# Clustered attention and its feed-forward layer on one core: rows of probabilities normalised before the float16 split instead of after the product with the values

## The chip, the cores and the metric

The kernel runs on one core of a Trainium2 chip. Its measure is the device time of one launch in microseconds (us); three runs of the kernel before gave 845.54, 847.42 and 848.62 us, a median of 847.42 us. Beside the timed runs there is one execution that was taken with the hardware profiler.

The core has five engines that run side by side, each through a queue of its own in a fixed order: TensorE (PE, matrix products; PEld is its loading of weights), VectorE (DVE), ScalarE (ACT), GpSimd (POOL) and SyncE (SP, which only issues DMAs here). An instruction that needs another engine's result waits on a semaphore, and all that is queued behind it on its engine waits with it.

## The reference

Four batches with 8 heads, 768 tokens and 64 features per head go through an attention in which a query sees only the keys of its own cluster, and then through a feed-forward layer of width 2048.

```python
q_assign = np.argmax(einsum(q / (norm(q) + 1e-6), c / (norm(c) + 1e-6)))   # 16 clusters per head; k_assign alike
scores = scale * q @ k.T                                                    # scale = 64 ** -0.5
scores = np.where(q_assign == k_assign, scores, -1e9)
attn = np.exp(scores - scores.max(-1))
attn = attn / (attn.sum(-1) + 1e-9)
x = attn @ v                                                                # heads side by side: 3072 x 512
h = x @ w_in                                                                # 512 x 2048
g = np.where(h >= 1, h, np.where(h <= -1, 0, (h + 1) ** 2 / 4))
out = g @ w_out                                                             # 2048 x 512
```

## The kernel before

**Tiling.** Queries go in 12 units u: batch b (4) times chunk c (3 chunks of 256 queries). A unit has 4 pairs of heads (hp), and a pair has 4 score steps n (2 heads times 2 tiles of 128 queries). A score step is four products of 128x384 on TensorE into the PSUM tile `pair0`: two of queries by keys, two that add a large penalty where the clusters differ (`at_scores`). VectorE takes the 128x768 scores out of PSUM with the row's bound in the same pass (`sS<-pair`, followed by a short read of its accumulator, `sbi`).

**Softmax.** In `at_soft`, ScalarE computes the exponential of those 768 columns in place and its row sum (`rs`), and then casts the result to float16 (`hl[:, 0]`); GpSimd subtracts this from the float32 values and so gets the lower half (`hl[:, 1]`). A DMA transposes both halves into `pT`. The very first unit keeps float32 and transposes on TensorE (`whole`). The three buffers of `sS` are used in turn, and so are three of `hl` and three of `pT`.

**Sum rows.** The row sums are applied after the product with the values. When the four sums of a pair of heads are there, `at_sums` takes 1/(sum + 1e-9) on ScalarE and VectorE and splits it in two float16 columns on GpSimd (`rr`). In `at_av`, eight small products of 128 columns on TensorE (`banka<-idu,rr`) spread these columns over the partitions into half of the PSUM bank `bank_a`, and 36 products of 256 columns (`banka<-pT,kv`) form attention times values in the other half. ScalarE copies the spread sums out (`rb<-banka`), VectorE multiplies the two (`rb<-banka,rb`), ScalarE casts the result to float16 (`X[u][:, 0]`), and GpSimd subtracts for the lower half (`X[u][:, 1]`). X is what the feed-forward products read; its buffers are named x, wk and word.

**Phi.** Queries and keys are scaled by powers of two before their float16 split. In `q_pairs`, four short VectorE instructions find a bound and a factor phi that brings the queries of a pair of heads in line with it; GpSimd multiplies the natural queries by phi (`qn<-qn,phi`) and ScalarE the transposed ones (`q<-q,phi`), each once per pair of heads and unit, 48 times in all.

**Feed-forward.** A unit has 8 groups f: 24 products of 256 columns into one of three PSUM banks (`bankh`, `banki`, `bankj`), two VectorE passes of 512 columns, a square, a cast and a subtraction on ScalarE and GpSimd, and 12 products of 512 columns into `pair1`. The groups of one unit run between the attention of later units.

**Norm of the centroids.** At the start `centroids` takes the norm with ScalarE's square root, and a tiny exponential behind it brings the table of the exponential back for all that follows.

**What sets the order.** The code records every instruction with a step; `Recorder.issue` turns this into one order by a planner: a backward pass gives each instruction a priority, a table of numbers (`NUDGES`) changes these, and `forward` then plays the engines with prices for each instruction and writes the order out. So the order of the instructions on all engines is fixed when the kernel is built, and a change of the code or of the table moves instructions everywhere.

Of the kernel before, what the change touches and what calls it, by code (L numbers as in the profile page):

```python
# [9 lines left out]
F16 = mybir.dt.float16  # L10
# [14 lines left out]
UNIT = 2.0**-10  # L25
EXP_MASK2 = 0x7F000000
# [20 lines left out]
BASE = 20  # L47
NUDGES = (
# [56 lines left out]
)  # L105
TILED = 248

def mix(a):  # L110

    a &= 0xFFFFFFFF
    a ^= a >> 16
    a = a * 0x7FEB352D & 0xFFFFFFFF
    a ^= a >> 15
    a = a * 0x846CA68B & 0xFFFFFFFF
    return a ^ a >> 16
# [1348 lines left out]
```

## Time and profile before

| | |
|---|---|
| median of three runs | 847.42 us (845.54 to 848.62) |
| span of the profiled execution | 844.9 us |
| PE busy | 807.8 us, 96% |
| PEld busy | 563.2 us, 67% |
| ACT busy | 667.1 us, 79% |
| DVE busy | 628.9 us, 74% |
| POOL busy | 528.7 us, 63% |
| granted clock of TensorE, mean | 0.994 |

The profiled execution has no timed value of its own in the answers: its span from the first to the last instruction is 844.9 us, 2.5 us under the median of the timed runs and inside a microsecond of the fastest. Work outside the span and the scatter of the runs lie in that difference.

How to read the rows below: a group names what an instruction writes and what it reads by the program's tile names (out<-in), with the number of partitions and elements. "busy" is the union of its time, "mean ns" the mean duration of one. Two instructions of one engine can overlap by some tens of ns, so durations add up to more than the busy time of the engine. Nearly all instructions stand under one line, since one helper issues them; the tile names tell them apart.

### The profile page before, as it was taken

Reading aid. Unit: us, or ns where it says so; the run is one execution under the profiler, and the core shown is the slowest. Engines: PE = TensorE matmul, PEld = TensorE weight load, DVE = VectorE, ACT = ScalarE, POOL = GpSimd, SP = SyncE. Lnnn points to the kernel's source line nnn. Section 1 sums busy time; section 2 is a strip of 40 time slices with the busy share of each in tenths; the row PEclk is TensorE's granted clock in tenths of the full one; section 3 lists DMA queues with packets and bytes.
Section 4 is the critical chain, followed back from the end, with each engine's and each line's share of the span. In section 5 each row is a group of like instructions: output and inputs, shape, how many; then the busy total and the mean of one; then the engine's idle time right before and its main releaser. Section 6 shows DMA issues by size and latency. Waiting matters only on the chain.

```text
span 844.9 us, 18910 instructions
## 1 busy us (share of the span) xinstructions
PE 807.8 (96%) x7100; PEld 563.2 (67%) x7100; DVE 628.9 (74%) x1390; ACT 667.1 (79%) x1175; POOL 528.7 (63%) x510
## 2 busy tenths in 40 slices
PE   2677999999999999999999999999999999999998
PEld 2455677667676767666666767666676676667776
DVE  5999998788888758669888758678888767454331
ACT  7889999999988778788778778788778778776332
POOL 1012589888878668666667667666757668666312
PEclk9999999999999999999999999999999999999999
DMA  9977898979999799889999979999988767666100
GB/s 313 295 187 179 241 225 192 182 156 198 207 170 183 149 160 175 173 181 207 203 159 179 157 149 175 188 189 193 212 161 145 154 135 141 129 128 103 24 26 26
DMA packets 404907, 142.50 MB, mean 169 GB/s; under 512 B 372816, under 2 KB 396624, under 8 KB 404816
## 3 DMA queue, kind: packets, MB, share of 16 engines
q1 hardware_dynamic: 404816, 141.30, 82.0%
q8 instruction: 55, 0.90, 0.4%
q14 instruction: 36, 0.29, 0.1%
HBM read 40.40 MB, written 6.29 MB: 55 GB/s over the span
## 4 chain that ended last, share of the span: by engine, by line
PE 85%; DVE 6%; issue 2%; DMA 1%; ACT 1%; POOL 1%; SPq 0%; DVEq 0%; POOLq 0%; ACTq 0%
PE pair L405 42%; PE banka L405 12%; PE bankj L405 11%; PE banki L405 11%; PE bankh L405 9%; DVE sS L405 1%; DMA kv<-n 1%; DVE w L405 1%; DVE bankj L405 1%; DMA pT<-hl 1%; POOL hl L405 0%; DVE wk L405 0%; DVE x L405 0%; DVE mx L405 0%; DVE bankh L405 0%
## 5 line engine op out<-in xcount | busy, mean ns | idle before, releaser
L405 POOL TENSOR_TENSOR hl<-sS,hl 128x768 f16<-128x768 f32 x176 | 299.0, 1702 | 118.3 <-ACT hl L405 99.0
L405 PE MATMUL pair<-w,g 128*128 128x512 f16 (+2 forms) x1120 | 275.9, 387 | 0.0
L405 DVE CUSTOM_DVE_ANT_0 sS<-pair,zero,er 128x768 f32<-128x768 f32 x192 | 194.4, 1013 | 71.5 <-PE pair L405 57.7
L405 PEld LDWEIGHTS <-w 128*128 128x128 f16 x2112 | 205.6, 98 | 41.2 <-issue 2.0
L405 ACT ACTIVATE sS<-sS,sbi 128x768 f32<-128x768 f32 x192 | 179.1, 933 | 67.5 <-DVE sbi L405 64.9
L405 PEld LDWEIGHTS <-g 128*128 128x128 f16 x1104 | 105.5, 98 | 101.8 <-issue 1.4
L405 PE MATMUL pair<-kv,q 128*128 128x384 f16 x768 | 159.7, 332 | 5.6 <-ACT pT L405 3.3
L405 ACT CAST hl<-sS 128x768 f16<-128x768 f32 x176 | 144.7, 826 | 7.8 <-DMA pT<-hl 5.6
L405 POOL TENSOR_TENSOR g<-r,g 128x512 f16<-128x512 f32 x80 | 95.8, 1198 | 54.7 <-ACT g L405 54.5
L405 PEld LDWEIGHTS <-q 128*128 128x128 f16 x992 | 78.7, 98 | 62.8 <-issue 20.4
L405 PE MATMUL banka<-pT,kv 128*64 128x256 f16 (+1 forms) x1680 | 104.8, 279 | 0.0
L405 PEld LDWEIGHTS <-kv 128*64 128x64 f16 (+1 forms) x1824 | 92.6, 108 | 6.5 <-DMA kv<-n 2.6
L405 ACT ACTIVATE r<-r,f_ra,f_rs 128x512 f32<-128x512 f32 x80 | 64.8, 810 | 25.4 <-DVE r L405 24.8
L405 PE MATMUL bankj<-x,w 128*128 128x256 f16 (+1 forms) x424 | 58.3, 289 | 0.9 <-DVE r L405 0.9
L405 ACT CAST g<-r 128x512 f16<-128x512 f32 x80 | 48.9, 611 | 8.1 <-DVE r L405 7.1
L405 POOL TENSOR_TENSOR qn<-qn,phi 128x256 f16<-128x256 f16 x48 | 31.7, 676 | 36.3 <-DVE phi L405 27.2
L405 PE MATMUL bankh<-x,w 128*128 128x256 f16 (+1 forms) x376 | 46.7, 277 | 0.0
L405 PE MATMUL banki<-x,w 128*128 128x256 f16 (+1 forms) x288 | 40.0, 290 | 0.0
L405 ACT ACTIVATE q<-q,phi 128x512 f16<-128x512 f16 x48 | 33.6, 717 | 5.0 <-DVE phi L405 4.9
L405 PE MATMUL banki<-wk,w 128*128 128x256 f16 x312 | 37.2, 273 | 0.0
L405 ACT ACTIVATION_READ_ACCUMULATOR sS<-sS,sbi 128x1 f32 x192 | 36.1, 188 | 0.0
L405 POOL CAST rr<-rs 128x4 f16<-128x4 f32 x48 | 13.2, 276 | 36.1 <-DVE bankh L405 13.7
(269 smaller groups left out, 1114.8 us busy)
## 6 DMA issues: line engine op xcount, KB each, us to landing
w<-in_moe_w_out_dram SPq DMA_DIRECT2D x14, 512.0 KB, 5.8
q<-in_q_dram SPq DMA_DIRECT2D x12, 512.0 KB, 4.8
kv<-in_k_dram SPq DMA_DIRECT2D x16, 384.0 KB, 4.3
kv<-in_v_dram SPq DMA_DIRECT2D x16, 384.0 KB, 4.6
out_dram<-o SPq DMA_DIRECT2D x11, 512.0 KB, 3.6
w<-in_moe_w_in_dram SPq DMA_DIRECT2D x10, 512.0 KB, 7.3
word<-in_moe_w_in_dram SPq DMA_DIRECT2D x6, 512.0 KB, 6.0
o<-in_v_dram SPq DMA_DIRECT2D x8, 384.0 KB, 4.0
```

The costliest lines, as they stand in the source:

```text
L405: fn(*args, **kw)
```

## The change

Four things are done, and the planner's table is another one.

- **Batches 1 to 3, softmax** (`at_soft`): behind the exponential, ScalarE scales the one row sum of this step (128x1), VectorE takes its reciprocal (128x1) and multiplies the 768 float32 probabilities by it in place (`NORM = "dddd"` gives all four steps of a pair to VectorE); only then come the float16 cast on ScalarE and the subtraction on GpSimd. The factor 2^15 (`WIDE`) is taken out again behind the product.
- **Batches 1 to 3, values** (`at_av`): no sums per pair (`at_sums`), no eight spreading products. ScalarE writes `X[u][:, 0]` straight from PSUM, and VectorE writes `X[u][:, 1]` as the product less that. `PAIRS = 1` leaves one pair of heads per call, as before. Batch 0 stays as it was.
- **Chunks 1 and 2 of every batch** (`q_scale`, `q_pairs`): no phi. The bound goes into the scale of the queries by two short VectorE instructions in `q_scale`, and one VectorE copy (128x16x64 float16) takes the place of the phi products. Chunk 0 of each batch keeps phi, so 16 of the 48 products on each of GpSimd and ScalarE stay.
- **Centroids**: the norm comes from three Newton steps on VectorE (128x1 each), and the exponential's table is loaded at once, so one table load is left.
- **Buffers**: `wk` and `word`, which serve the weights early on, become one tile `late`; from batch 1 on, two more buffers for `pT` lie in it, five in all. The ring of X has four buffers where it had seven.
- **Order**: `NUDGES` and its hash go, `SHIFTS` adds one number per recorded call to the priorities, and the backward pass is repeated 31 times instead of 20.

```diff
-BASE = 20
-NUDGES = (
...
+WIDE = 2.0**15
+NORM = "dddd"
+PAIRS = 1
+BASE = 31
+SHIFTS = (
+    -300, 6196, 4613, 9761, -1686, 3724, 8146, 5319, 7315, -16432, -1123, 6379, -15621, -10423, -3454, 2074, -3225,
...
-        for seed in NUDGES:
-            self.nudge(seed, prio)
+        names = sorted({x.ev for x in self.nodes})
+        shift = dict(zip(names, SHIFTS, strict=True))
+        for x in self.nodes:
+            prio[x] += shift[x.ev]
...
-    wk = tiles("wk", 2, 4096)
-    word = tiles("word", 1, 8192)[0]
-    rings["w32"], rings["x"] = Ring(wk[:1] + rings["o"].bufs), Ring(tiles("x", 3, 4096) + wk + [word[:, :1024], word[:, 1024:]])
+    late = tiles("late", 1, 16384)[0]
+    wk, word = [late[:, :1024], late[:, 1024:2048]], late[:, 2048:]
+    rings["w32"], rings["x"] = Ring(wk[:1] + rings["o"].bufs), Ring(tiles("x", 3, 4096) + [late[:, 3072:]])
...
-    rec.scalar.activation(out=tab, in_=ones[:, :1], func=AF.Sqrt)
+    rec.scalar.activation(out=tab, in_=ones[:, :1], func=AF.Exp, scale=0.0)
...
-        nrm = const.tile([P, 1], F32, name="c_nrm")
-        rec.scalar.activation(out=nrm, in_=ss, func=AF.Sqrt)
-        rec.scalar.activation(out=tab, in_=nrm, func=AF.Exp, scale=0.0)
-        rn = const.tile([P, 1], F32, name="c_rn")
-        rec.vector.tensor_scalar(out=rn, in0=nrm, scalar1=1e-6, scalar2=None, op0=ALU.add)
+        (rn, y), m = (const.tile([P, 1], F32, name=f"c_{x}") for x in ("rn", "y")), tab
+        rec.vector.tensor_scalar(
+            out=y.bitcast(U32), in0=ss.bitcast(U32), scalar1=-0.5, scalar2=float(0x5F3759DF), op0=ALU.mult, op1=ALU.add
+        )
+        for _ in range(3):
+            rec.vector.scalar_tensor_tensor(out=m, in0=y, scalar=ss, in1=y, op0=ALU.mult, op1=ALU.mult)
+            rec.vector.tensor_scalar(out=m, in0=m, scalar1=-0.5, scalar2=1.5, op0=ALU.mult, op1=ALU.add)
+            rec.vector.tensor_tensor(out=y, in0=y, in1=m, op=ALU.mult)
+        rec.vector.tensor_scalar(out=rn, in0=ss, scalar1=y, scalar2=1e-6, op0=ALU.mult, op1=ALU.add)
...
+        if u % NCH:
+            f = BX[u // NCH]
+            es = e["es"] = new("es", [NP], F32, 2)
+            rec.vector.scalar_tensor_tensor(
+                out=iv, in0=f["sk"], scalar=ES_MIN / QK, in1=iv, op0=ALU.mult, op1=ALU.max
+            )
+            rec.vector.scalar_tensor_tensor(
+                out=es, in0=f["ik"], scalar=-QK, in1=iv, op0=ALU.mult, op1=ALU.mult
+            )
...
-        raw, es, ri = (ps[:, i * NP : i * NP + m] for i in range(3))
+        if c:
+            es = e["es"][:, pairs]
+            rec.vector.tensor_copy(nat[:, x, 0], nat[:, x, 1])
+        else:
+            raw, es = (ps[:, i * NP : i * NP + m] for i in range(2))
...
-            e["pT", j] = new("pT", [2 * T, CT, P], F16, 3)
+            new("pT", [2 * T, CT, P], F16, 3)
+            if b:
+                if "late" not in rings:
+                    rings["late"] = Ring(rings["pT"].bufs + [late[:, :1536], late[:, 1536:3072]])
+                rings["late"].i += 1
+                e["pT", j] = view(rings["late"].last(), [2 * T, CT, P], F16)
+            else:
+                e["pT", j] = view(rings["pT"].last(), [2 * T, CT, P], F16)
...
+        if b:
+            r = e["rs"][:, n : n + 1]
+            rec.scalar.activation(out=r, in_=r, func=AF.Copy, scale=1 / WIDE, bias=1e-9 / WIDE)
+            rec.vector.reciprocal(r, r)
+            who = NORM[n]
+            if who == "d":
+                rec.vector.tensor_scalar(out=sf, in0=sf, scalar1=r, scalar2=None, op0=ALU.mult)
+            elif who == "a":
+                rec.scalar.activation(out=sf, in_=sf, func=AF.Copy, scale=r)
+            else:
+                rec.gpsimd.tensor_tensor(out=sf, in0=sf, in1=r.to_broadcast([P, S]), op=ALU.mult)
-        at_sums(e, n)
+        if not b:
+            at_sums(e, n)
...
-    def at_av(b, hp, c):
-        pv, rb = bank_a[:, :CQ], bank_a[:, CQ:]
+    def at_av(b, hps, c):
+        u, n = b * NCH + c, len(hps)
+        es, kvs = [A.pop((b, hp, c)) for hp in hps], [KV[b, hp] for hp in hps]
+        pv = bank_a[:, : n * CQ].rearrange("p (n q) -> p n q", q=CQ)
+        rb = bank_a[:, CQ:].rearrange("p (n q) -> p n q", q=CQ)
+            for x, e in enumerate(() if b else es):
+            for x, (e, kv) in enumerate(zip(es, kvs)):
-        rs = new("rb", [CQ], F32)
...
+        to = slice(hps[0], hps[-1] + 1)
+        if hps[0] == 0:
+            X[u] = new("x", [NP, CQ], F32) if u == 0 else new("x", [2, NP, CQ], F16)
+        if b:
+            rec.scalar.activation(out=X[u][:, 0, to], in_=pv, func=AF.Copy, scale=1 / WIDE)
+            rec.vector.scalar_tensor_tensor(
+                out=X[u][:, 1, to], in0=pv, scalar=1 / WIDE, in1=X[u][:, 0, to], op0=ALU.mult, op1=ALU.subtract
+            )
+            return
+        rs = new("rb", [n, CQ], F32)
         rec.scalar.copy(rs, rb)
-        if hp == 0:
-            X[u] = new("x", [NP, CQ], F32) if u == 0 else new("x", [2, NP, CQ], F16)
         if whole(b, c):
             rec.vector.scalar_tensor_tensor(
-                out=X[u][:, hp], in0=pv, scalar=1 / UNIT, in1=rs, op0=ALU.mult, op1=ALU.mult
+                out=X[u][:, to], in0=pv, scalar=1 / UNIT, in1=rs, op0=ALU.mult, op1=ALU.mult
             )
             return
         rec.vector.tensor_tensor(out=rs, in0=pv, in1=rs, op=ALU.mult)
-        rec.scalar.copy(X[u][:, 0, hp], rs)
-        rec.gpsimd.tensor_tensor(out=X[u][:, 1, hp], in0=rs, in1=X[u][:, 0, hp], op=ALU.subtract)
+        rec.scalar.copy(X[u][:, 0, to], rs)
+        rec.gpsimd.tensor_tensor(out=X[u][:, 1, to], in0=rs, in1=X[u][:, 0, to], op=ALU.subtract)
```

Three places in the order show what moved. The first is TensorE at the first pair of heads of batch 2; `rr` are the split reciprocal sums, `idu` a scaled identity, `kv` the values, `pT` and `late` the transposed probabilities. Before:

```order
L405 MATMUL pair_79<-kv_62,q_65 128x384
L405 LDWEIGHTS rr_157
L405 MATMUL banka<-idu,rr_157 64x128
...
L405 LDWEIGHTS kv_61
L405 MATMUL banka<-pT_152,kv_61 64x256
L405 LDWEIGHTS kv_61
L405 MATMUL banka<-pT_153,kv_61 64x256
```

And in the changed kernel:

```order
L382 MATMUL pair_77<-kv_62,q_65 128x384
L382 LDWEIGHTS g_74
L382 MATMUL pair_78<-w_76,g_74 128x512
...
L382 LDWEIGHTS kv_61
L382 MATMUL banka<-late_69,kv_61 64x256
L382 LDWEIGHTS kv_61
L382 MATMUL banka<-pT_150,kv_61 64x256
```

The eight products with `rr` (seven more stand behind the one shown, each with its load) are gone; six feed-forward products stand between the last score step and the values. Over the whole program TensorE issues 288 products and 288 loads less, and nothing else on it changes in number.

The second place is VectorE around the first score steps of batch 2, `sS` being the scores, `rs` the row sums, `r` the feed-forward passes, `bankj`, `zs`, `mx`, `kv` and `aq` the preparation of later keys and queries. Before:

```order
L405 TENSOR_TENSOR er_139<-bankj,zm_143 128x4
L405 SCALAR_TENSOR_TENSOR n_77<-kv_63,sc_135,n_77 128x12x64 [waits DMAHW3_49,DMAHW0_49,Activation_49]
L405 TENSOR_TENSOR rb_160<-banka,rb_160 128x256 [waits Activation_49]
L405 ISA sS_86,sbi_147<-pair_79,zero,er_139 128x768 [waits PE_49,Pool_49]
L405 ISA sbi_147 128x1
L405 TENSOR_SCALAR qn_67<-zs_137 128x4x16 [waits Pool_49]
L405 TENSOR_REDUCE aq_125<-q_66 128x4 [waits DMAHW2_49]
L405 TENSOR_SCALAR r_205<-banki,f_lo_181,f_hi_176 128x512 [waits DVE_49,PE_49]
L405 SCALAR_TENSOR_TENSOR kv_63<-kv_63,sv_166 128x768 [waits DMAHW4_49,DVE_49,Activation_49]
L405 SCALAR_TENSOR_TENSOR r_205<-banki,f_gs_201,r_205 128x512 [waits Activation_49]
L405 TENSOR_REDUCE kv_63<-bankj 128x192 [waits DVE_49,PE_49]
L405 RECIPROCAL rs_148<-rs_148 128x4 [waits Activation_49]
```

And in the changed kernel:

```order
L382 TENSOR_TENSOR er_137<-bankj,zm_141 128x4
L382 RECIPROCAL rs_146<-rs_146 128x1
L382 RECIPROCAL rs_146<-rs_146 128x1 [waits Activation_49]
L382 TENSOR_SCALAR sS_85<-sS_85,rs_146 128x768 [waits DVE_49]
L382 TENSOR_SCALAR r_205<-banki,f_lo_181,f_hi_176 128x512 [waits PE_49,Pool_49]
L382 TENSOR_SCALAR qn_67<-zs_135 128x4x16 [waits Pool_49]
L382 RECIPROCAL rs_146<-rs_146 128x1 [waits Activation_49]
L382 TENSOR_SCALAR sS_84<-sS_84,rs_146 128x768
L382 SCALAR_TENSOR_TENSOR r_205<-banki,f_gs_201,r_205 128x512 [waits Activation_49]
L382 TENSOR_REDUCE kv_63<-bankj 128x192 [waits PE_49]
L382 SCALAR_TENSOR_TENSOR x_71<-banka,x_71 128x256 [waits Activation_49]
L382 TENSOR_REDUCE mx_136<-kv_63 128x12 [waits DVE_49]
```

Between the passes that were there stand a reciprocal of one column and a multiply of 768 columns for each score step, and the multiply of a step does not follow its reciprocal's exponential at once: other passes lie between.

The third place is ScalarE at the start, from the first scaled query tile to the first copies out of PSUM. Before:

```order
L405 ACTIVATE qn_67<-q_65,sq_128 128x4x64 [waits DMAHW0_49,DVE_49]
L405 ACTIVATE qn_67<-q_65,sq_128 128x4x64 x3
L405 ACTIVATE n_77<-kv_61,sc_135 128x12x64 [waits DVE_49,Activation_49]
L405 ACT_TABLE_LOAD
L405 ACTIVATE tab<-c_nrm 128x1 [waits Activation_49]
L405 COPY q_65<-pair_79 128x1024 [waits PE_49]
```

And in the changed kernel:

```order
L382 ACTIVATE qn_67<-q_65,sq_126 128x4x64 [waits DMAHW1_49,DVE_49]
L382 ACTIVATE qn_67<-q_65,sq_126 128x4x64 x3
L382 ACTIVATE n_75<-kv_61,sk_130 128x12x64 [waits DVE_49,Activation_49]
L382 ACTIVATE o_68<-w_76 128x1024 [waits DMAHW5_49,DMAHW4_49]
L382 COPY q_65<-pair_77 128x1024 [waits PE_49]
```

The second table load and the tiny exponential in front of the first copy are gone, and one pass over a weight tile stands there instead. On SP, the load of the centroids now stands ahead of the first load of queries, where it stood behind it.

## Rows read from the trace of the kernel before

**Rows 1.** The page's forty slices of the span: busy tenths of PE, and TensorE's clock.

```profile
PE   2677999999999999999999999999999999999998
PEclk9999999999999999999999999999999999999999
```

**Rows 2.** Busy us of each engine (instructions) in six stretches; clock, DMA, GB/s.

```profile
75.00:100.00 25.00, 21.18 (x173) 14.87 (x168) 25.00 (x44) 24.18 (x39) 8.98 (x8) 1.00 0.87 236
100.00:125.00 25.00, 25.00 (x147) 17.46 (x146) 23.61 (x35) 24.50 (x41) 20.73 (x13) 1.00 0.96 211
217.00:404.00 187.00, 185.79 (x1687) 129.20 (x1686) 147.08 (x334) 153.67 (x279) 135.61 (x126) 1.00 0.93 179
404.00:593.00 189.00, 189.00 (x1723) 130.92 (x1721) 147.17 (x340) 150.81 (x278) 130.32 (x126) 1.00 0.93 177
593.00:694.00 101.00, 101.00 (x907) 70.29 (x905) 80.15 (x189) 78.44 (x143) 65.53 (x64) 1.00 0.84 162
694.00:779.00 85.00, 85.00 (x749) 58.22 (x748) 47.12 (x91) 65.00 (x119) 60.32 (x58) 1.00 0.67 125
```

**Rows 3.** Timeline of PE at one `at_av`: start us, us, engine, instructions.

```profile
412.61 0.81 PE L405 MATMUL pair<-kv,q 128*128 128x384 f16 x4
413.35 0.41 PE L405 MATMUL banka<-idu,rr 128*64 128x128 f16 x8
413.60 2.13 PE L405 MATMUL banka<-pT,kv 128*64 128x256 f16 x36
```

**Rows 4.** Groups by form: count | busy us, mean ns | idle before, releaser.

```profile
L405 PE MATMUL banka<-idu,rr 128*64 128x128 f16 x384 | 20.0, 227 | 0.0
L405 ACT COPY rb<-banka 128x256 f32<-128x256 f32 x48 | 17.3, 361 | 5.5 <-PE banka L405 5.1
L405 ACT ACTIVATE rs<-rs 128x4 f32<-128x4 f32 x48 | 9.7, 201 | 0.1
L405 ACT ACTIVATE q<-q,phi 128x512 f16<-128x512 f16 x48 | 33.6, 717 | 5.0 <-DVE phi L405 4.9 <-PE banki L405 0.2
L405 POOL CAST rr<-rs 128x4 f16<-128x4 f32 x48 | 13.2, 276 | 36.1 <-DVE bankh L405 13.7 <-DVE rs L405 12.5 <-PE pair L405 9.6
L405 POOL TENSOR_TENSOR x<-rb,x 128x256 f16<-128x256 f32 x20 | 15.6, 778 | 2.3 <-ACT x L405 1.3 <-DVE phi L405 1.0
L405 POOL TENSOR_TENSOR qn<-qn,phi 128x256 f16<-128x256 f16 x48 | 31.7, 676 | 36.3 <-DVE phi L405 27.2 <-ACT sS L405 8.7 <-issue 0.2
L405 POOL TENSOR_TENSOR hl<-sS,hl 128x768 f16<-128x768 f32 x176 | 299.0, 1702 | 118.3 <-ACT hl L405 99.0 <-ACT rs L405 5.4 <-DVE r L405 3.8
L405 ACT ACTIVATE sS<-sS,sbi 128x768 f32<-128x768 f32 x192 | 179.1, 933 | 67.5 <-DVE sbi L405 64.9 <-POOL g L405 0.6 <-DVE rs L405 0.5
L405 DVE RECIPROCAL rs<-rs 128x4 f32<-128x4 f32 x48 | 8.3, 172 | 13.1 <-ACT rs L405 12.8
```

**Rows 5.** DVE instructions of three tiles: ns least/median/most, first and last start.

```profile
L405 DVE TENSOR_SCALAR wk<-wk x3: 678/679/2050, 90.2 to 137.8; 128x1024 uint32<-128x1024 uint32 x3
L405 DVE SCALAR_TENSOR_TENSOR qn<-q,sq,qn x48: 455/478/1619, 9.4 to 682.5; 128x256 f16<-128x256 f32 x48
L405 DVE SCALAR_TENSOR_TENSOR kv<-kv,sv x12: 985/1265/1665, 197.3 to 623.8; 128x768 f16<-128x768 f32 x12
```

**Rows 6.** Timeline of DVE and POOL at 515 us.

```profile
515.12 1.64 POOL L405 TENSOR_TENSOR hl<-sS,hl 128x768 f16<-128x768 f32 x1
515.25 1.80 DVE L405 TENSOR_TENSOR banki<-zs,has 128x256 f32<-128x256 f32 x1
516.97 0.41 DVE L405 TENSOR_TENSOR rb<-banka,rb 128x256 f32<-128x256 f32 x1
517.30 0.41 DVE L405 TENSOR_REDUCE zm<-banki 128x16 f32<-128x256 f32 x1
```

**Rows 7.** Timeline of PE and ACT at the start.

```profile
9.96 1.89 PE L405 MATMUL pair<-idf,qn 128*128 128x128 bf16 x16 [2.02 <-DVE qn L405]
11.42 1.28 ACT L405 ACT_TABLE_LOAD   x1
12.82 1.91 ACT L405 COPY q<-pair 128x1024 bf16<-128x1024 bf16 x2
```

More of the change, by code (lines that the diff above doesn't have):

```diff
@@ L375, in backward @@
         return start
-    def nudge(self, seed, prio):
-        a = mix(seed * 2654435761 + 1)
-        b = mix(a + 1)
-        c = mix(b + 1)
-        names = sorted({x.ev for x in self.nodes})
-        lo, every, size = b % len(names), (1, 2, 5)[(a >> 8) % 3], float(500 << ((a >> 16) % 5))
-        at = {y: i for i, y in enumerate(names)}
-        for x in self.nodes:
-            i = at[x.ev]
-            if lo <= i < lo + (1 << (a % 8)) and not (i - lo) % every:
-                r = c if c >> 8 & 1 else mix(c + i * 7919)
-                prio[x] += ((r & 0xFFFF) / 32768.0 - 1.0) * size
     def issue(self):
@@ L1093, in at_sums @@
             rec.gpsimd.tensor_tensor(out=rh[:, 1], in0=rr, in1=rh[:, 0], op=ALU.subtract)
-    def at_av(b, hp, c):
-        u = b * NCH + c
-        e, kv = A.pop((b, hp, c)), KV[b, hp]
-        pv, rb = bank_a[:, :CQ], bank_a[:, CQ:]
-        with rec.group():
-            for t in range(CT):
-                for a in range(2):
+    def at_av(b, hps, c):
[3 more added lines that the diff above has]
+        rb = bank_a[:, CQ:].rearrange("p (n q) -> p n q", q=CQ)
+        with rec.group():
+            for x, e in enumerate(() if b else es):
+                for t in range(CT):
+                    for a in range(2):
+                        for j in range(2):
+                            i = j * CT + t
+                            rec.tensor.matmul(
+                                rb[j * D : (j + 1) * D, x, t * P : (t + 1) * P],
+                                e["rr"][:, a, i : i + 1].to_broadcast([P, D]),
+                                idu,
+                                start=(a == 0),
+                                stop=(a == 1),
+                            )
+            for x, (e, kv) in enumerate(zip(es, kvs)):
+                for kc in range(T if whole(b, c) else 0):
@@ L1121, in at_av @@
-            for kc in range(0 if whole(b, c) else T):
-                for i, (va, pa) in enumerate(((0, 0), (0, 1), (1, 0))):
-                    for j in range(2):
-                        pT = e["pT", j].rearrange("p (a n) t q -> p a n (t q)", a=2)[:, pa, kc]
-                        rec.tensor.matmul(
-                            pv[j * D : (j + 1) * D],
-                            kv["vs"][:, va, j, kc * D : (kc + 1) * D],
-                            pT,
-                            start=(kc == 0 and i == 0),
-                            stop=(kc == T - 1 and i == 2),
-                        )
@@ L1132, in at_av @@
-        rs = new("rb", [CQ], F32)
+                            pv[j * D : (j + 1) * D, x],
+                            kv["v"][:, j, kc * D : (kc + 1) * D],
+                            e["pT", j][:, kc].rearrange("p t q -> p (t q)"),
+                            start=(kc == 0),
+                            stop=(kc == T - 1),
+                        )
+                for kc in range(0 if whole(b, c) else T):
+                    for i, (va, pa) in enumerate(((0, 0), (0, 1), (1, 0))):
+                        for j in range(2):
+                            pT = e["pT", j].rearrange("p (a n) t q -> p a n (t q)", a=2)[:, pa, kc]
+                            rec.tensor.matmul(
+                                pv[j * D : (j + 1) * D, x],
+                                kv["vs"][:, va, j, kc * D : (kc + 1) * D],
+                                pT,
+                                start=(kc == 0 and i == 0),
+                                stop=(kc == T - 1 and i == 2),
+                            )
@@ L1368, in at, with joined @@
         ev.setdefault(step, []).append((fn, args))
+    def joined(b, hp, c):
+        return 1 if not b or (b < B - 1 and c == NCH - 1 and hp < 2) else PAIRS
     wat = [WA + WR * ((i | 1) - 0.5) for i in range(2 * NF)]
@@ L1383, in tile_clustered_attention_moe @@
             else:
-                steps = [first(b - 1, hp, NCH - 1) + SC + LA - 3] + [s0 - x for x in (6, 5.6, 5, 4)]
+                m = joined(b - 1, hp, NCH - 1)
+                s1 = first(b - 1, hp // m * m + m - 1, NCH - 1)
+                steps = [s1 + SC + LA - 3 if m == 1 else s1 + LA - 0.4] + [s0 - x for x in (6, 5.6, 5, 4)]
+                if m == 2:
+                    steps[1:] = [s0 - x for x in (5.3, 5.1, 5, 4)]
             for x, fn in zip(steps, (kv_load, k_scale, k_split, v_split, k_assign)):
@@ L1400, in tile_clustered_attention_moe @@
                     at(s0 + n + 1, at_soft, b, hp, c, n // CT, n % CT)
-                at(s0 + LA - 0.5, at_av, b, hp, c)
+                m = joined(b, hp, c)
+                if hp % m == m - 1:
+                    at(s0 + LA - 0.5, at_av, b, range(hp + 1 - m, hp + 1), c)
             sf = max(sf, s0 + FA, wat[-1] + 3 if u else 0)
```

55 lines of the change are left out of this document (18 added, 37 removed), and 107 rows, old and new, of tables (NUDGES, SHIFTS).

## The prediction

> **What bounds the kernel now.** I read the slices of the page first. TensorE is at nine tenths or more from the fifth slice to the last, at the full granted clock [rows 1], so a product taken away there is time taken away, as long as something else doesn't run out. What that could be is asked of the windows, cut where the first score step of batch 1, 2 and 3 begins, in the middle of batch 3 and at the end of its scores [rows 2]. In the 187 us of batch 1 TensorE has 1.2 us of idle time, in the 375 us behind it none; VectorE is busy for 147.1 of 187 us (79%), ScalarE for 153.7 (82%), GpSimd for 135.6 (73%). So nobody else is at an end there, and the change moves work to VectorE, which has 40 us left per batch. The first two windows show how VectorE and TensorE get on when VectorE is full: at 23.6 of 25 us (94%) TensorE still had no idle time, at 25.0 of 25 it lost 3.8 us.
>
> **What goes from TensorE.** Each `at_av` issues its eight spreading products over 0.25 us: they start at 413.35, and the products with the values follow at 413.60 [rows 3]. Their 227 ns mean and the 0.41 us of the group [rows 3, 4] contain the pipeline's length, which the next group overlaps; the distance of the starts is the price. Batches 1 to 3 have 3 x 3 x 4 = 36 such calls: 36 x 0.25 = 9.0 us. All of it lies in stretches where TensorE hardly rests, and the order shows nothing added on TensorE. This term has little room: 8.7 to 9.3 us, by the hundredths in which the row is given.
>
> **What VectorE gets.** Per batch 48 multiplies of 768 float32 columns and 48 reciprocals in place of 12. No such multiply is in the trace. The nearest is the one-input pass from SBUF to SBUF over 1024 words of 32 bits: 678 ns at least and 679 in the median [rows 5]. In proportion to the columns that is 0.51 us for 768; with a fixed part of about 0.15 us (a short reciprocal takes 0.172 [rows 4]) it is 0.15 + 0.53 x 0.75 = 0.55 us, which I take. The upper end is the two-input pass over 768 columns, 0.985 us at least [rows 5]. Consecutive VectorE instructions overlap by 0.08 us: one starts at 516.97, lasts 0.41, and the next starts at 517.30 [rows 6]. So each multiply takes 0.47 us of the engine and each of the 36 extra reciprocals 0.09 us.
>
> To that comes waiting. At 515.25 a VectorE pass over 256 columns that reads two SBUF operands lasts 1.80 us, to the end of the GpSimd subtraction that began 0.13 us before it and 0.29 us on, while a pass of the same width with an operand in PSUM lasts 0.41 at 516.97 [rows 6]; the 1024-word pass has a case of 2050 ns too [rows 5]. The excess of the median over the least is 0.02 us for `qn` and 0.28 us for `kv` [rows 5]: these are my bounds for the mean wait of a multiply, and I take 0.15.
>
> The Trainium skill's page "SBUF — State Buffer", section "Who interferes with whom", says that such a one-input pass and a GpSimd instruction hold one pair of ports exclusively, each for its whole length, and whoever comes second waits. By that rule the row at 515 us is what must happen whenever the two meet, and the trace agrees; how often they meet the page doesn't say, and the sum would be the one below or that of the second rival's last sentence.
>
> In batch 1 VectorE then needs 147.1 + 48 x (0.47 + 0.15) + 36 x 0.09 = 180.1 us, of 187 - 12 x 0.25 = 184.0 us: 98%. In batch 2 it is 180.2 of 186.0 (97%), in the first half of batch 3 80.2 + 14.9 + 1.6 = 96.7 of 99.5 (97%), in the second 63.6 of 83.5 (76%). The order gives no relief: ahead of the last pair of heads of batches 1, 2 and 3 both orders have the same number of first-layer products (808, 1384, 1984), so the feed-forward was not pulled forward. If VectorE can be filled to 98%, nothing is lost. At 96% the three stretches become 187.6, 187.7 and 100.7 us, 6.5 us more. Nothing between 94 and 100% is in the trace; I take the middle, 3.2 us.
>
> **The other engines.** GpSimd loses, per batch, 12 times 0.276 and 0.778 and 8 products with phi of 0.676: 135.6 becomes 117.6 us, 64% [rows 2, 4]. ScalarE gets 48 x 0.20 for the row sums and loses 12 x (0.36 + 0.20) and 8 x 0.72: 151 us, no bound [rows 2, 4]. The correction that VectorE now makes from PSUM replaces a multiply from the same PSUM bank over the same columns; I cost it at nothing, as I do the short instructions and the copy that replace phi, eight units in all. The chain of each step grows by 0.20 + 0.17 + 0.55 + 0.15 = 1.07 us ahead of the cast. What hides this are the two more buffers for `pT` and the feed-forward products that stand between the scores and the values in the order; what it costs bare is in the third case. The multiply is one more instruction that everything behind it on VectorE waits for, the scores pass above all, and TensorE has only one PSUM tile for scores.
>
> **The start.** The table load of 1.28 us stands between the end of the transposes (9.96 + 1.89 = 11.85) and the copy at 12.82 [rows 7]: at most 0.97 us are to be had, and a weight pass stands in its place now. The Newton steps are ten short instructions more, at up to 0.17 us each. Bounds: 1.0 us won to 1.7 lost; I take 0.4 won, since the centroids are now loaded ahead of the queries, so that most of the steps lie before the queries land.
>
> **Sum.** 844.9 us of span - 9.0 - 0.4 + 3.2 = 838.7 us of span. The timed median stands 2.5 us above the profiled span, and I keep this: 841.2 us.
>
> **Rivals.**
> 1. Forecast: TensorE stays the bound, VectorE costs a few us. 841.2 us, with stalls of 0 to 6.5 us and the start's bounds 837 to 846. For it: 94% beside a full TensorE, and 18 us less on GpSimd per batch. Chance 0.60.
> 2. VectorE becomes the bound from batch 1 to the middle of batch 3, and the kernel gets slower. With a wait of 0.15 us and a VectorE that can be filled to 94.4% only, the stretches become 190.8, 190.9 and 102.4 us: 14.6 us of stalls, 847.4 - 9.4 + 14.6 = 852.6. With a wait of 0.28 and 96%, 194, 194 and 104 us: 22.5 us, 860.5. It decides once the stalls exceed 9.4 us. For it: a scores pass that comes late holds the only tile for scores. Against it: GpSimd's relief, and the fact that the present 79% contains waits that get shorter too. If the multiply ran at one column per cycle (0.985), VectorE would need 201 us in batch 1 and the time would be near 880. And if multiplies met GpSimd by chance, in 64% of cases and with half of its 1.70 us subtraction still to run [rows 4], the mean wait would be 0.54 us, the stretches 199, 199 and 106 us, and the time 872. Each of these last two has 0.04. Chance 0.23 in all.
> 3. The longer chain comes through: the probabilities of a pair arrive 1.07 us later, and if every fourth of the 36 value groups waits that out, 9 x 1.07 = 9.6 us are gone: 847, no change. For it: there are still three buffers for the scores, each held longer. Against it: 3.9 us between score steps (187/48), and TensorE has other products. Chance 0.17.
>
> **Numbers.** About 0.3%, 2.5 us, is what a measurement of this kernel can tell from no change. Faster by more takes nearly all of the first case and a little of the third: 0.62; no change 0.16, from the third and the edges of the others; slower 0.22, the second. The range goes from 835 us (no stall, the start at its best, a little left over) to 855 us, well into the second case.
>
> **What would show it.** Right: 288 products less on TensorE; no idle time worth more than 5 us on it between 217 us and the end of the scores; VectorE at 95 to 98% in batches 1 and 2; the multiply at 0.55 us at least and some 0.7 in the mean. Wrong in its size: TensorE waiting for VectorE's scores pass (`pair` behind `sS`) by more than 9 us; a multiply of over 0.9 us in the mean, with GpSimd's subtraction beside it each time; a value group that waits for the DMA of `pT`. The prediction fails if VectorE can't be kept busy beyond 94%.

## The result: slower by 0.5%, and the profile after

The kernel after takes 851.56 us in the median (850.26 to 852.0), the kernel before 847.61 us beside it; the ratio is 1.0054, interval [1.0039, 1.0069]. The prediction said 841.2 us. The profiled execution took 851.6 us, of which the span is 849.8: 4.9 us more than the 844.9 of before. First the page's busy times of the engines, and the slices of TensorE and VectorE:

```profile
PE 801.3 (94%) x6812; PEld 553.5 (65%) x6812; DVE 729.6 (86%) x1644; ACT 648.5 (76%) x1212; POOL 481.1 (57%) x370
...
PE   2677999999999999999999999999999999999998
...
DVE  6999998988999999889999899989999888777331
```

The 288 products are gone from TensorE (6812 instructions for 7100), and it is busy for 6.5 us less than the 807.8 of before; but its idle time grew from 37.1 to 48.5 us, by 11.4. -6.5 + 11.4 = +4.9. In tenths the row of PE reads as in [rows 1]; where the idle time lies is seen only in the windows. They are cut as in [rows 2], with the first score step of batch 1 now at 211 us:

```profile
75.00:100.00 25.00, 21.08 (x162) 15.29 (x159) 24.61 (x44) 23.28 (x37) 7.26 (x6) 1.00 0.82 203
...
211.00:404.00 193.00, 187.58 (x1619) 128.26 (x1617) 180.20 (x413) 153.35 (x304) 125.52 (x89) 1.00 0.90 175
404.00:593.00 189.00, 185.07 (x1585) 126.33 (x1585) 175.82 (x409) 145.27 (x288) 112.45 (x79) 1.00 0.88 169
593.00:694.00 101.00, 99.32 (x865) 69.36 (x860) 93.39 (x235) 75.25 (x152) 60.45 (x44) 1.00 0.87 167
```

The first two numbers are the window's length and TensorE's busy time: it lost 5.4, 3.9 and 1.7 us, 11.0 in all, where the three windows of before lost 1.2 [rows 2]. The third busy time is VectorE's: 180.2 of 193 us (93%), 93% and 92%. The clock is full in all of them. Batch 1 begins 5.9 us sooner than before, but part of that is order: 1514 products of TensorE stand ahead of it where 1544 stood.

What was added, by tile and by group (least/median/most ns; count | busy us, mean ns), answers to [rows 4, 5]:

```profile
L382 DVE TENSOR_SCALAR sS<-sS,rs x144: 590/619/2073, 220.7 to 788.1; 128x768 f32<-128x768 f32 x144
...
L382 POOL TENSOR_TENSOR hl<-sS,hl 128x768 f16<-128x768 f32 x176 | 300.9, 1718 | 168.3 <-ACT hl L382 87.4 <-issue 29.7 <-ACT rs L382 24.4
L382 ACT ACTIVATE rs<-rs 128x1 f32<-128x1 f32 (+1 forms) x156 | 30.8, 197 | 1.6
L382 DVE RECIPROCAL rs<-rs 128x1 f32<-128x1 f32 (+1 forms) x156 | 24.2, 156 | 14.9 <-ACT rs L382 14.5
```

The page gives the multiplies 117.9 us in all, 0.82 each. Taken one by one in the trace, 58 of the 144 overlap no instruction of GpSimd by more than 20 ns and last 0.610 us in the mean; the other 86 last 0.965. What TensorE waits for between 211 and 700 us (us in total, times, longest), and below it what the page's chain says:

```profile
PE pair L382 <- DVE sbi L382: 5.2, 10, 0.9
PE bankj L382 <- DVE r L382: 1.4, 2, 1.1
PE bankh L382 <- DVE r L382: 0.9, 1, 0.9
...
PE 54%; DVE 24%; ACT 8%; DMA 6%; issue 6%; POOL 1%; SPq 0%; DVEq 0%; ACTq 0%; POOLq 0%
```

All of the large waits end with VectorE. `sbi` is the last thing that the scores pass writes, so the first row is TensorE's next score step standing behind a late pass, ten times for half a microsecond. One such case in the timeline (start us, us; the stretch answers to [rows 6]):

```profile
243.50 1.01 DVE L382 CUSTOM_DVE_ANT_0 sS<-pair,zero,er 128x768 f32<-128x768 f32 x1
244.44 0.08 DVE L382 DVE_READ_ACCUMULATOR2_ANT sbi<- 128x1 f32 x1
244.44 1.54 DVE L382 TENSOR_SCALAR sS<-sS,rs 128x768 f32<-128x768 f32 x1
245.91 1.63 DVE L382 TENSOR_SCALAR qn<-zs 128x64 f16<-128x64 f32 x1
247.46 0.80 DVE L382 TENSOR_SCALAR r<-bankj,f_lo,f_hi 128x512 f32<-128x512 f32 x1
...
249.02 1.01 DVE L382 CUSTOM_DVE_ANT_0 sS<-pair,zero,er 128x768 f32<-128x768 f32 x1
...
243.90 1.16 POOL L382 TENSOR_TENSOR g<-r,g 128x512 f16<-128x512 f32 x1 [1.03 <-issue]
245.00 0.58 POOL L382 MEMSET n<- 128x576 f16 x1
245.73 3.35 POOL L382 TENSOR_TENSOR hl<-sS,hl 128x768 f16<-128x768 f32 x2 [0.16 <-ACT hl L382]
...
250.09 0.81 PE L382 MATMUL pair<-kv,q 128*128 128x384 f16 x4 [0.64 <-DVE sbi L382]
```

VectorE has no gap here. The multiply at 244.44 takes 0.93 us over its median, the 64-column instruction behind it 1.63 us, both beside GpSimd; the scores pass comes at 249.02, and TensorE stands still for 0.64 us until it is through.

### The profile page after: what moved, and what is told of

Same layout as the page of the kernel before. It is cut to its first block, busy times and chain, and to the rows that moved or that the text cites. A ratio compares the mean times of both kernels' runs of the same rounds, so it can differ in the third digit from the quotient of the medians.

```text
span 849.8 us, 18428 instructions
## 1 busy us (share of the span) xinstructions
PE 801.3 (94%) x6812; PEld 553.5 (65%) x6812; DVE 729.6 (86%) x1644; ACT 648.5 (76%) x1212; POOL 481.1 (57%) x370
## 4 chain that ended last, share of the span: by engine, by line
PE 54%; DVE 24%; ACT 8%; DMA 6%; issue 6%; POOL 1%; SPq 0%; DVEq 0%; ACTq 0%; POOLq 0%
PE pair L382 26%; DVE sS L382 10%; PE banka L382 8%; PE bankj L382 7%; PE banki L382 7%; PE bankh L382 5%; DVE r L382 3%; ACT sS L382 2%; DMA kv<-in_k_dram 2%; DMA pT<-hl 2%; DVE qn L382 1%; DMA kv<-n 1%; ACT hl L382 1%; DVE w L382 1%; DVE bankj L382 1%
## 5 line engine op out<-in xcount | busy, mean ns | idle before, releaser
L382 PE MATMUL pair<-w,g 128*128 128x512 f16 (+2 forms) x1120 | 272.8, 387 | 0.0
L382 PE MATMUL pair<-kv,q 128*128 128x384 f16 x768 | 157.3, 328 | 10.6 <-DVE sbi L382 5.4
L382 DVE TENSOR_SCALAR sS<-sS,rs 128x768 f32<-128x768 f32 x144 | 117.9, 822 | 1.3
L382 PE MATMUL banka<-pT,kv 128*64 128x256 f16 (+1 forms) x1176 | 90.6, 282 | 0.0
L382 PE MATMUL banki<-x,w 128*128 128x256 f16 (+1 forms) x600 | 76.8, 281 | 1.9 <-DVE w L382 1.1
L382 PE MATMUL bankj<-x,w 128*128 128x256 f16 (+1 forms) x568 | 74.9, 285 | 1.4 <-DVE r L382 1.4
L382 PE MATMUL bankh<-x,w 128*128 128x256 f16 (+1 forms) x496 | 61.5, 276 | 0.0
L382 PE MATMUL banka<-late,kv 128*64 128x256 f16 x504 | 45.2, 274 | 0.5 <-DVE late L382 0.2
L382 POOL TENSOR_TENSOR w<-late,w 128x1024 f16<-128x1024 f32 x16 | 36.6, 2290 | 0.9 <-ACT w L382 0.6
L382 DVE RECIPROCAL rs<-rs 128x1 f32<-128x1 f32 (+1 forms) x156 | 24.2, 156 | 14.9 <-ACT rs L382 14.5
```

Of the source, the lines that this page charges most:

```text
L382: fn(*args, **kw)
```

## The experiments

The theories were: VectorE has become too full, by its own work and by the time that it is held up beside GpSimd (theory A, the second rival); the longer chain from the exponential to `pT` comes through (theory B, the third rival); or the loss lies in the new order or in other parts of the change (theory C). Runs 1 to 3, 5 to 7, 9 and 10 keep the order of the kernel after, instruction by instruction, and change only operands, pieces or form. In runs 2 and 9 the spare tile also takes the place of a small buffer of batch 0 (`rb`). All were run beside the kernel before, which took 847.1 to 847.5 us; each ratio is to that.

**1. The multiply on 64 columns.**

```diff
+                fn, args, kw = rec.nodes[-1].calls[-1]
+                rec.nodes[-1].calls[-1] = fn, args, dict(kw, out=sf[:, :64], in0=sf[:, :64])
```

> The changed kernel with its order kept instruction by instruction, but each multiply on VectorE works on 64 of the 768 columns, so the other columns stay undivided. Theory A (VectorE is full: 117.9 us of multiplies put it at 92 to 96% and TensorE waits for its passes): the idle time of TensorE between the scores of batch 1 and the end of the scores falls from 11.0 us to 2 or less, and the time from 851.6 to 838 to 841 us. Theory B (the chain from the exponential to the cast is longer): three of its four added pieces stay (0.20 row sum, 0.16 reciprocal, the hand-overs), so at least half of the loss stays: 846 to 849 us. Theory C (the loss lies in the new order or in the other parts): 850 us or more.

845.49 us, ratio 0.9978 [0.9969, 0.9988].

```profile
L382 DVE TENSOR_SCALAR sS<-sS,rs x144: 222/250/1735, 220.3 to 783.2; 128x64 f32<-128x64 f32 x144
...
211.00:404.00 193.00, 190.07 (x1642) 130.18 (x1641) 167.30 (x420) 154.29 (x308) 123.82 (x90) 1.00 0.92 179
```

With 0.37 us less in the median the multiply still has cases of 1.7 us. The columns are worth 6.1 us of time. TensorE's idle time in the three windows falls from 11.0 to 6.9 us, not to 2: the result lies between what theory A and theory B expected, and the rest is left to the next runs.

**2. The multiply beside the chain.** It is made in full, but into a tile that nobody reads, so the cast doesn't wait for it.

```diff
+                fn, args, kw = rec.nodes[-1].calls[-1]
+                rec.nodes[-1].calls[-1] = fn, args, dict(kw, out=spare.bitcast(F16)[:, :S])
```

> The same order again; VectorE multiplies all 768 columns, but writes them as float16 to a tile that nobody reads, so the cast and the subtraction no longer wait for the multiply (the probabilities stay undivided). VectorE's load stays, provided the multiply lasts as long as before (0.82 us in the mean, to be read from the trace). Theory A: no gain, 849 to 853 us. Theory B: the chain is short again, 839 to 843 us. Theory C: 850 us or more.

850.78 us, ratio 1.0047 [1.003, 1.0064]: as the kernel after.

```profile
L382 DVE TENSOR_SCALAR spare<-sS,rs 128x768 f16<-128x768 f32 x144 | 124.8, 866 | 1.6
```

The load didn't quite stay: the multiply takes 0.87 us in the mean where it took 0.82, and VectorE is busy for 734.7 us, 5.1 more. At run 1's rate (46.6 us less of VectorE for 6.1 us of time) that would hide some 0.7 us, an estimate. So the chain through the multiply is worth 1 or 2 us at most, not the 9.6 of the third rival; the added row sum and reciprocal are still in it here, and theory C is not touched by this run.

**3. GpSimd's subtraction on 64 columns.**

```diff
+        if b:
+            fn, args, kw = rec.nodes[-1].calls[-1]
+            rec.nodes[-1].calls[-1] = fn, args, dict(out=hl[:, 1, :64], in0=sf[:, :64], in1=hl[:, 0, :64], op=ALU.subtract)
```

> The same order; GpSimd's subtraction behind the cast works on 64 of 768 columns from batch 1 on (the lower halves of the probabilities are left out), so GpSimd is busy for far less time and a multiply seldom meets it. Theory A with the lock as its main part (mean wait 0.21 us, 30 us in all): the multiply falls from 0.82 to 0.62 us, VectorE to some 88 to 90%, and the time to 839 to 843 us. Theory A without the lock (the bare 0.61 us would be enough to fill it): 847 to 851 us. Theory B: the chain to the transposing DMA gets 1.5 us shorter, 840 to 845 us. Theory C: 850 us.

840.5 us, ratio 0.9923 [0.9908, 0.9938].

```profile
PE 800.4 (95%) x6812; PEld 554.0 (66%) x6812; DVE 698.8 (83%) x1644; ACT 646.8 (77%) x1212; POOL 287.3 (34%) x370
L382 DVE TENSOR_SCALAR sS<-sS,rs 128x768 f32<-128x768 f32 x144 | 101.2, 706 | 1.4
...
211.00:404.00 193.00, 191.14 (x1660) 131.99 (x1659) 173.71 (x429) 157.03 (x311) 65.89 (x91) 1.00 0.93 180
```

Nothing was taken from VectorE, and it is busy for 30.8 us less: so long had it been held up beside this subtraction. 16.7 us of that are the multiplies', the rest other passes'. The multiplies still take 0.71 us in the mean, not the expected 0.62, since they go on meeting GpSimd's other work. The time is 11.1 us less than after.

**4. One step in four normalised by ScalarE**, the planner run again with the same table.

```diff
-NORM = "dddd"
+NORM = "ddad"
```

> One multiply of four goes to ScalarE (the third step of each pair of heads), all else as in the changed kernel; the planner makes another order of it. VectorE loses 36 multiplies (30 us), ScalarE gets 36 of about 0.93 us and goes from 79 to 85% in batches 1 and 2. Theory A: TensorE's idle time in the scores' stretch falls below 5 us, 843 to 847 us. Theory B: the chain stays as long or gets longer, 850 to 853 us. Theory C: the new order decides, anything from 845 to 858 us.

918.7 us, ratio 1.0845 [1.0809, 1.0882]. VectorE has less to do (723.2 us) and TensorE's idle time is 89 us of the span: with this set of calls the table gives a far worse order. The run says nothing on theories A and B.

**5 and 6. The subtraction in two and in four pieces**, so that a hold is shorter.

```diff
+        if b:
+            fn, args, kw = rec.nodes[-1].calls.pop()
+            for x in range(2):    # in run 6 a 4 stands for each 2 of these two lines
+                y = slice(x * S // 2, (x + 1) * S // 2)
+                rec.nodes[-1].calls.append((fn, args, dict(out=hl[:, 1, y], in0=sf[:, y], in1=hl[:, 0, y], op=ALU.subtract)))
```

> The changed kernel in its own order on TensorE, VectorE and ScalarE; from batch 1 on, each of GpSimd's subtractions behind the cast is issued as two of 384 columns instead of one of 768. All arithmetic is kept. Theory A, the lock with GpSimd as the cause: a multiply that meets GpSimd has at most half as long to wait, so the mean multiply falls from 0.82 to some 0.72 us and the time from 851.6 to 845 to 848 us. If only the sum of GpSimd's time counted, or VectorE's load without the waits, nothing changes: 850 to 853 us.

> The same with four subtractions of 192 columns. Theory A: the mean multiply falls to some 0.68 us, time 843 to 847 us; each further instruction costs GpSimd some tens of ns, which it has (57% busy). Without the lock as cause: 850 to 854 us.

Halves: 851.66 us, 1.0052 [1.0034, 1.0069]. Quarters: 861.43 us, 1.0161 [1.0129, 1.0192]. First run 5, then run 6:

```profile
L382 DVE TENSOR_SCALAR sS<-sS,rs 128x768 f32<-128x768 f32 x144 | 113.5, 792 | 1.3
...
211.00:404.00 193.00, 186.52 (x1606) 127.06 (x1604) 177.45 (x409) 152.37 (x301) 132.71 (x133) 1.00 0.90 172
```


```profile
L382 POOL TENSOR_TENSOR hl<-sS,hl x608: 536/548/2717, 87.8 to 800.7; 128x192 f16<-128x192 f32 x144, 128x768 f16<-128x768 f32 x8
L382 DVE TENSOR_SCALAR sS<-sS,rs x144: 590/620/1585, 220.7 to 797.2; 128x768 f32<-128x768 f32 x144
...
211.00:404.00 193.00, 186.04 (x1600) 126.87 (x1599) 174.87 (x407) 151.67 (x300) 148.56 (x223) 1.00 0.91 171
...
DVE sS L382 <- POOL hl L382: 14.9, 23, 1.3
```

Both missed what theory A expected. In halves the multiply gets only 0.03 us shorter, not 0.10, VectorE is busy for 4.1 us less in all, and the time is that of the kernel after. So shorter holds in themselves gained nothing here, and this run speaks against the length of a single hold as the cause. In quarters the multiply does get shorter (0.744 us in the mean), but four pieces take 2.3 us where one took 1.72. GpSimd falls behind, and a new wait stands in the last row: the scores pass waits for GpSimd to give back a scores buffer, 14.9 us between 211 and 700 us, 4.3 in halves, 1.8 in the kernel after.

**7. A multiply that is never held up.** It writes an accumulator as well.

```diff
+                fn, args, kw = rec.nodes[-1].calls[-1]
+                rec.nodes[-1].calls[-1] = fn, args, dict(kw, scalar2=0.0, op1=ALU.add, accum_out=spare)
```

> The same order; each multiply also writes out an accumulator, which nobody reads, to take it out of the form that goes at two columns per cycle. I expect about 0.9 us for each whether or not GpSimd runs, and a read of the accumulator of 0.08 us, so VectorE gets 144 x 0.16 = 23 us more load than with 0.82, but no multiply waits. Theory A, waits in one piece of up to 1.6 us as the cause: 843 to 849 us. Theory A, load as the cause: 856 us or more, with VectorE at 97% or more in batches 1 and 2.

870.3 us, ratio 1.0268 [1.0245, 1.0291].

```profile
L382 DVE TENSOR_SCALAR_CACHE_REDUCE sS<-sS,rs x144: 982/1004/1015, 220.0 to 806.7; 128x768 f32<-128x768 f32 x144
...
211.00:404.00 193.00, 180.39 (x1528) 122.09 (x1527) 184.84 (x437) 147.38 (x292) 117.35 (x84) 1.00 0.84 165
404.00:593.00 189.00, 183.69 (x1588) 125.85 (x1586) 181.87 (x445) 140.96 (x280) 108.75 (x78) 1.00 0.87 168
```

No case is 15 ns over the median, so nothing holds this form up; but it is 0.39 us longer than the bare multiply, and VectorE is at 96% in both windows. TensorE then loses 12.6 and 5.3 us: load alone is enough for a loss, and waits in one piece are not needed for it. The prediction had VectorE fuller still, at 97 to 98%, for 3.2 us.

**8. The planner told that the multiply is 80 ns longer**, the order made anew.

```diff
-            return 68 + n / 0.96 / fast + ...
+            return 68 + n / 0.96 / fast + ... + 80 * (n == 768 and fast == 2)
```

> The changed kernel with the planner's price of the multiply raised by 80 ns, to the 0.61 us that it takes undisturbed; the planner makes another order from the same table. If its low price were the reason for an order that does not hold, this should gain: 845 to 850 us. If the table fits one order only, as the run with one multiply on ScalarE makes likely, it is far slower: 870 us or more.

959.4 us, ratio 1.1316 [1.1263, 1.137]: as in run 4, another order, from a table that was fitted to the order of the kernel after.

**9. The hold without the chain.** The 64 columns that the transposing DMA waits for come first, the other 704 go into a tile that nobody reads.

```diff
+            rec.nodes[-1].calls[-1] = fn, args, dict(out=hl[:, 1, :64], in0=sf[:, :64], in1=hl[:, 0, :64], op=ALU.subtract)
+            rec.nodes[-1].calls.append(
+                (fn, args, dict(out=spare.bitcast(F16)[:, :704], in0=sf[:, 64:], in1=hl[:, 0, 64:], op=ALU.subtract)))
```

> The order of the kernel after, kept instruction by instruction. From batch 1 on GpSimd's subtraction behind the cast is made first on 64 of the 768 columns, and only on this the transposing DMA waits; then GpSimd makes the other 704 into a tile that nobody reads (so the lower halves of the probabilities are left out). GpSimd keeps its work and its meetings with VectorE, but a step's chain is some 1.3 us shorter. If GpSimd gives back its time in the run with the narrow subtraction because its steps' chain gets shorter (pT comes sooner, so the products with the values do), this comes near that run: 840 to 844 us, with GpSimd busy near 500 us. If it is the meetings on VectorE, and GpSimd's fullness, it stays at 850 to 856, with VectorE busy near 729 us and the multiply at 0.8 us in the mean.

849.7 us, ratio 1.0026 [1.0015, 1.0037].

```profile
PE 802.8 (95%) x6812; PEld 553.8 (65%) x6812; DVE 729.4 (86%) x1644; ACT 648.1 (76%) x1212; POOL 505.9 (60%) x514
...
211.00:404.00 193.00, 187.79 (x1621) 128.62 (x1620) 180.93 (x413) 153.99 (x304) 132.71 (x135) 1.00 0.89 176
```

With a shorter chain and GpSimd as busy, 1.9 of run 3's 11.1 us are won; VectorE is as full as after, TensorE loses as much in batch 1 (8.6 us in the three windows, for 11.0 after), and the rest stays.

**10. Both narrow** (edits 1 and 3).

> The order of the kernel after, kept. From batch 1 on both the multiply of VectorE and the subtraction of GpSimd are made on 64 of 768 columns (the other probabilities are not divided, and their lower halves left out). If VectorE's fullness and GpSimd's hold are two separate losses, they add up: 851.6 - 6 - 11 = 834 to 836 us, which is the time the prediction's terms give with no stall at all (its 844.9 - 9.4 + 2.5 = 838.0). If they are one loss told twice (VectorE too full, by its own columns or by waits), one of the two is enough and this stays at 838 to 841 us. VectorE near 650 us busy, TensorE's idle time in batches 1 to 3 under 3 us.

839.69 us, ratio 0.9911 [0.9892, 0.9931].

```profile
211.00:404.00 193.00, 192.62 (x1669) 132.70 (x1667) 159.50 (x432) 156.69 (x311) 60.86 (x91) 1.00 0.94 182
```

The two don't add up. The four runs as a table:

| | subtraction on 64 columns | on 768 |
|---|---|---|
| multiply on 64 columns | 839.69 us | 845.49 us |
| multiply on 768 | 840.5 us | 851.56 us (after) |

The multiply's columns cost 0.8 us where the subtraction is narrow, within the runs' scatter, and 6.1 where it is whole. Apart they cost 0.8 and 5.8 us, together 11.9: 5.3 us arise only where both are there. (The 838.0 us that the expectation names is the time with no stall, and 834 to 836 lies below it; with TensorE's idle time at 0.9 us in the three windows, nothing more was to be had.)

**11 and 12. No fitted order**, after and before: `prio[x] += 0 * shift[x.ev]`, and `NUDGES[:0]`.

> The kernel after with its table of shifts multiplied by zero: the planner sets the order by its rules alone. It sizes what the fitted order is worth, and with the next run what the edit would do between two orders that nobody fitted. If the edit costs time by VectorE's load in any order, this is slower than the next run by more than the 0.5% between the fitted two; if the fitted orders decide the difference, the two can stand in either sequence. I expect 900 to 960 us, as the two runs with the table on an order that it wasn't fitted to (918.7 and 959.4).

> The kernel before with an empty list of nudges: the planner sets the order by its rules alone. I expect it slower than the 847.6 us of the kernel before, by 2 to 10%, as the order is then fitted to nothing: 865 to 930 us. Its distance to the run before it tells what the edit does without a fitted order: if the edit itself is a loss, this one is the faster of the two by more than 4 us.

862.78 us, 1.0193 [1.0149, 1.0236], and 865.31 us, 1.0213 [1.0191, 1.0235]. The first is far better than I expected. The intervals overlap: between two orders that nobody fitted, this edit makes no difference that these runs can tell, and the sign named for an edit that is a loss in itself (before faster by more than 4 us) didn't come. The fitted order is worth 11.2 us after and some 18 before.

## Why the prediction was wrong

**The step that failed** is the stall term: "If VectorE can be filled to 98%, nothing is lost. At 96% ... 6.5 us more ... I take the middle, 3.2 us." TensorE lost 9.8 us more in the three windows than before, and VectorE came to 92 to 93%. That is the second rival's mechanism, and the prediction's own line "The prediction fails if VectorE can't be kept busy beyond 94%" is what happened. That the rival's 852.6 us (worked out with 94.4%) is so near is in part luck: it has 14.6 us of stalls and 9.4 won, where idle time grew by 11.4 us and TensorE's busy time fell by 6.5. The sign that the prediction named, TensorE waiting for the scores pass by more than 9 us, came to 5.2; the rest are waits for other results. The upper bound of the term, 6.5 us at 96%, was too low as well: run 7, with VectorE at 96, 96 and 92%, lost 23.7 us in the three windows. The evidence for the middle was two windows of 25 us at the start, one at 94% without a loss and one at 100% with 3.8 us [rows 2]; a stretch that short says little of a whole batch with a fixed order on every engine. The runs in the order of the kernel after show what was missing (batch 1, 193 us from 211 us on, and batch 2, 189 us from 404 us on; VectorE's busy time, and what TensorE lost):

| run | batch 1: VectorE | TensorE idle | batch 2: VectorE | TensorE idle |
|---|---|---|---|---|
| 10, both narrow | 159.5 us, 83% | 0.4 us | 153.6 us, 81% | 0.0 us |
| 1, multiply narrow | 167.3, 87% | 2.9 | 163.7, 87% | 2.9 |
| 3, subtraction narrow | 173.7, 90% | 1.9 | 169.0, 89% | 0.6 |
| 6, quarters | 174.9, 91% | 7.0 | 171.5, 91% | 3.6 |
| 5, halves | 177.5, 92% | 6.5 | 175.5, 93% | 2.1 |
| 2, multiply aside | 178.8, 93% | 6.8 | 177.7, 94% | 7.1 |
| after | 180.2, 93% | 5.4 | 175.8, 93% | 3.9 |
| 9, hold without chain | 180.9, 94% | 5.2 | 176.4, 93% | 1.4 |
| 7, never held up | 184.8, 96% | 12.6 | 181.9, 96% | 5.3 |

The loss grows with VectorE's share, but the share alone doesn't set it: at 92 to 94% it goes from 1.4 to 7.1 us. Run 6 has the wait for the buffers. Run 2's row is of an execution that took 856.0 us, 5 us over the run's median. Run 1 loses more than run 3 with less on VectorE; that a hold of up to 1.7 us at the wrong place costs more than the same time spread evenly would explain it, but no run shows that.

**VectorE's load.** 180.1 us were predicted for batch 1 and 180.2 measured, but that agreement is luck. For batch 2 it was 180.2 against 175.8, for the half of batch 3 96.7 against 93.4, so over the three windows the forecast was 7.6 us too high. And its parts were off: the bare multiply takes 0.610 us where I took 0.55. By the undisturbed ones on 64 columns (0.246, run 1) and on 768 a column costs 0.52 ns, as I took, but the fixed part is 0.21 us and not 0.15. The mean wait is (0.965 - 0.610) x 86 / 144 = 0.21 us where I took 0.15, inside the bounds. What offsets it is overlap: in batch 1 the durations of VectorE's instructions add up to 207.0 us, 43.9 more than before, while its busy time grew by 33.1; so overlap took back 10.7 us more than before, where 84 x 0.08 = 6.7 stand in the prediction. VectorE's work was thus sized too high, if anything, and what it would do to TensorE far too low.

**GpSimd's meetings.** Batch 1 has GpSimd busy for 65% of the window, and 60% of all multiplies met it, near the 64% of the second rival's last sentence. But a meeting costs 0.355 us, not half of 1.70. The Trainium skill's page "SBUF — State Buffer", section "Who interferes with whom", says that the one that issues first holds the ports for its whole length and the other waits; the trace agrees. In 16 of the 88 meetings (with those under 20 ns) the multiply was first; it then lasts 0.63 us in the mean, and seven subtractions beside it take 1.65 to 1.92 us for 1.65. In 72 GpSimd was first: 48 of the 49 multiplies among these that last over 0.7 us end 0.41 to 0.42 us behind an instruction of GpSimd, so one that comes within the last 0.2 us of it loses nothing. And only 39 of the 72 begin beside the subtraction; most others meet work of 0.6 to 1.3 us. What I missed is that these holds are not a price per multiply only: run 3 gave back 30.8 us of VectorE, in the stretch where it had nothing to spare, and 14 of them not at the multiplies. In the kernel before, GpSimd's subtraction was the same and VectorE at 79%, and TensorE lost 1.2 us.

**TensorE's saving** of 9.0 us: its busy time fell by 6.5 us after, and by 8.8 (807.8 to 799.0) in run 10, where next to nothing stalls. Run 10's figure bears the term out; where 2.3 us more stand as busy in the kernel after, I did not work out. The start: the query copy begins at 11.77 us instead of 12.82 [rows 7], 1.05 us sooner and so a little over the bound of 0.97, since the transposes too begin 0.55 us sooner, at 9.41; what the start won in all can't be told from the order's shift. With no stall the prediction's sum is 844.9 - 9.4 + 2.5 = 838.0 us; runs 3 and 10 took 840.5 and 839.7.

**The third rival** is refuted by run 2 for the multiply's own part in the chain, the largest of the four; runs 3 and 10, in which the row sum and the reciprocal stay, leave little room for the rest (839.7 us in run 10, 838.0 with no stall).

**What stays open.** Run 3 takes the hold away and also two fifths of GpSimd's work (481.1 to 287.3 us). Run 9 speaks against the steps' own chain as the reason, and VectorE waits for GpSimd's results for 3.2 us only (1.8 for `hl`, 1.4 for `g`, between 211 and 700 us) in the kernel after, which speaks for the hold; but no run takes the meetings away and leaves both GpSimd's work and VectorE's own load as they are, and halving the hold (run 5) gained nothing. And 0.5% is less than a fitted order is worth: the fit gained some 7 us more before than after, more than the 4 us between the two kernels. So what is shown is that, in this order, VectorE's load and holds cost the time; whether a longer search would find an order that bears this load was not tried. No complete version here beats the kernel before; run 3 would, but it leaves out the lower halves of most probabilities.

## What to carry over

Don't price an engine that another one waits for at fixed places as free until it is full. Here TensorE lost 0 to 3 us per batch with VectorE at 81 to 90%, 1.4 to 7.1 at 91 to 94%, and 5.3 and 12.6 at 96%, so a move onto such an engine needs a loss in its sum well before 100%. Count into its load the time that it is held up beside the other engine, from the least and the mean of each group, and look for the hold's owner: here work left out on GpSimd gave back more time than work left out on VectorE. And where an order is fitted to one set of calls, compare unfitted with unfitted before the edit itself is judged.

## What the runs showed of the hardware

- The multiply with an accumulator takes 1004 ns in the median and at most 1015, plus 81 ns for reading the accumulator; without, 619 in the median and up to 2073. The section "Who interferes with whom" of the Trainium skill's page "SBUF — State Buffer" says that the form which writes its accumulator doesn't enter the contended mode; the trace agrees.
- GpSimd's subtraction takes at least 295, 536, 904, 1510 and 1633 ns for 64, 192, 384, 704 and 768 columns (runs 9, 6, 5, 9, after): by the first and the last a fixed part of 173 ns, not the "some tens of ns" of run 6's expectation, and 1.90 ns per column. By these least times, cutting it in four costs 0.5 us.
- Held up is not only what is large: a VectorE instruction over 64 columns took 1.63 us beside the subtraction, where 11 of its 16 cases take 0.17 to 0.21.
